# Sliding-window attention into a two-layer MLP: the first four blocks' biases on TensorE, and a new order of the first loads

## The chip, the cores and the metric

The kernel runs on one core of a Trainium2 chip. The metric is the device time of one execution in microseconds (us); each execution is timed, and the median of the runs stands for the kernel. One further execution was profiled.

## What is computed

Attention with 8 batches, 8 heads, 576 positions and a head size of 64, in which a query sees itself and the 127 positions before it, with a linear bias on the distance (ALiBi); then a two-layer MLP with a squared ReLU over the 4608 tokens. Inputs and output are float32.

```python
scores = scale * np.matmul(q, k.transpose(0, 1, 3, 2))        # scale = 1/8
rel = pos[:, None] - pos[None, :]
slopes = 2.0 ** (-8.0 * (np.arange(H) + 1) / H)
bias = slopes[:, None, None] * (-np.abs(rel))[None, :, :]
mask = (rel >= 0) & (rel < 128)
scores = np.where(mask, scores + bias[None], -1e9)
attn = softmax(scores)
x = (attn @ v) as [4608, 512]
h = x @ w_in                                                  # w_in [512, 2048]
r = np.maximum(h, 0.0)
out = (r * r) @ w_out                                         # w_out [2048, 512]
```

## The kernel before

**Tiling.** The 576 positions of a batch are cut into four blocks of 128 and one of 64, so there are 40 blocks. A block's queries need its own keys (the diagonal part) and those of the block before (the other part of the window). The first block of each batch has the diagonal part alone; these eight are blocks 0 to 7, done first. Blocks 0 to 3 are jobs of their own, 4 and 5, and 6 and 7, share one. The rest follow by pairs of batches: six full blocks, then two half blocks in one job.

**One block.** k and q of a block land side by side in a `kq` tile (128 positions by 1024). Both are transposed so that head channels lie on partitions: for blocks 0 to 7 by TensorE (`tp`, L470) with an eviction to `kqf` by ScalarE or VectorE (L291, L289), for later blocks by a DMA transpose that SP issues (`kqT`, L456). TensorE then writes scores to `s` (L526), keys on partitions and queries in columns, two heads at a time in two row groups. ScalarE writes `P` = exp(scale * s) (L550) in four instructions, VectorE multiplies `P` by `masks` (L558), which hold exp of the bias or 0. TensorE multiplies `P` by v with a column of ones (`pv`, L593, two halves of four heads); VectorE takes the reciprocal of the sum (L611) and scales (L615) into `x`. `x` is transposed into `xT`, by TensorE (`xp`, L635) for blocks 0 to 7 and by an SP DMA (L623) after.

**The MLP.** Nine groups of 512 tokens. For each, `h` (L718 for groups 0 to 2, whose units are 128 or 256 tokens wide, L735 after), then ReLU on ScalarE (`rt`, L683), the square on VectorE (`g`, L692), and `o` (L762), whose four parts of the hidden dimension need the four quarters of w_out in turn. A result tile `osb` is stored by SP (L786). `h` and `o` have two PSUM banks each, so only two output tiles are open at a time.

**Loads.** POOL issues the loads that cast float32 to bfloat16: blocks' k and q (L414), v (L419), w_in in four quarters of columns (L360), w_out in four quarters of rows (L363). `FIRST` gives their order at the start: block 0, 1, 2, w_in 0 and 1, w_out 0, block 3, w_in 2 and 3, and so on. Block 0's k and q (`N_HW = 1`) come another way: SP and ScalarE's queue load float32 halves into `stage` (L397) and VectorE casts them to `kq`.

**Order.** A planner in the kernel's own Python orders every instruction: each task has engines with a cost, a key, dependences, slots that it takes from rings and frees, and for a DMA a transfer time; the planner always starts the task that can start first on its engine, the key deciding within `NEAR` ns, and `ADJ` shifts single keys. Instructions are emitted in that order and each engine runs its own in order. Where the plan sees TensorE idle over 200 ns, `fill` puts matmuls on a zero tile `warm` there (L270).

Of the kernel before, what the change touches and what calls it, by code (L numbers as in the profile page):

```python
# [15 lines left out]
FIRST = ["b0", "b1", "b2", "i0", "i1", "o0", "b3", "i2", "i3", "o1", "o2", "o3", "b4", "b5", "b6", "b7"]  # L16
DIAG = [[0], [1], [2], [3], [4, 5], [6, 7]]
N_HW = 1
N_PE = 8
N_CUT = 1  # L20
N_PVH = 0
N_WARM = 8
FILL = 0.7
LEAD = 720
# [3 lines left out]
UNITS = {0: [(0, 128, 4), (128, 128, 4), (256, 128, 4), (384, 128, 4)], 1: [(0, 256, 2), (256, 256, 2)],  # L28
         2: [(0, 256, 2), (256, 256, 2)]}
PIECES = [4, 4, 4, 4]  # L30
# [5 lines left out]
    "e1.2": 99737.5, "e14.1": 197.91, "e16.2": -128.81, "e19.2": -8999803.95, "e2.3": -401.4, "e20.1": 2.03,  # L36
    "e3.1": 99809.35, "e6.3": 99108.3, "fc3.1": -547.61, "fc3.2": -237.14, "fc3.3": -684.14, "fc3.5": -652.43,
    "fc3.7": -100007.3, "fc3.8": -9000379.3, "m18.2": 165.47, "m18.3": -239.22, "n1.1": 100203.0, "n10.1": 495.17,
    "n12.1": 587.74, "n15.0": 308.11, "n16.0": 356.11, "n16.1": 706.81, "n9.0": 332.79, "o0.2.0": -103.48,
    "o0.2.1": -122.14, "o0.2.2": -99562.6, "o1.0.1": -100260.7, "o1.0.2": -100228.4, "o1.1.1": -99628.0,  # L40
    "o1.1.2": -152.7, "o1.1.3": -198.1, "o1.3.1": -99940.7, "o2.0.1": -99143.6, "o2.1.1": 200, "o2.2.0": -615.0,
    "oe1.0.0": -220.3, "ones2": 99179.7, "pv11.1": -99297.74, "pv19.0": -100068.55, "r18.0": 267.47, "r3.1": 99545.79,
    "relufc3.1": -100188.3, "relufc3.5": -99571.3, "reluu0.0.2": -99848.1, "reluu0.1.0": -100044.0,
    "reluu1.1.4": -579.61, "reluu2.0.5": -282.54, "squ0.0.0": -100027.7, "squ1.1.3": -388.31, "squ2.1.1": 40,
    "u0.2.0": -8999828.5, "u0.2.1": -99868.0, "u1.1.0": 39, "u1.1.1": -99305.4, "u1.1.4": -99991.3,
    "u1.1.6": -99367.7, "u2.0.5": -99873.0, "u2.0.6": -468.21, "u2.0.7": -99687.4, "u2.1.1": -187.45,
    "u2.1.2": -482.59, "u2.1.3": 39, "u2.1.7": -266.7,
# [24 lines left out]
class Plan:  # L72


    LAT = {"PE": 210.0, "ACT": 60.0, "DVE": 80.0, "POOL": 200.0, "SP": 200.0, "ACTQ": 200.0}
    BEGIN = {"POOL": 840.0, "SP": 740.0, "ACTQ": 740.0, "ACT": 2550.0, "DVE": 860.0, "PE": 1190.0}
# [4 lines left out]
    NEAR = {"PE": 25, "ACT": 60, "DVE": 25}  # L81
# [17 lines left out]
    def order(self):  # L99
# [37 lines left out]
        while len(done) < n_all:  # L137
# [40 lines left out]
            for u in t.users:  # L178
                left[u] -= 1
                at = st + dur if u.engs.keys() == {e} and t.dma is None else t.end  # L180
                if "SP" in u.engs and t.dma is None:
                    at += self.TO_SP
                u.ready = max(u.ready, at)
                if not left[u]:
                    for x in u.engs:
                        cand[x].append(u)
# [6 lines left out]
def kernel(  # L193
# [44 lines left out]
    masks = const.tile([128, H, 2, 128], BF16)  # L238
    dist = const.tile([128, 2, 128], FP32)
# [35 lines left out]
    def act(n):  # L275
        return n * 0.95 + 115.0

    def dve(n, rate=1):
        return n / rate / 0.96 + 180.0

    def dve_p(n, rate=1):
        return n / rate / 0.96 + 185.0
# [31 lines left out]
    t_ident = plan.add({"DVE": 230.0}, EARLY + 1, build_ident, [t_iota], name="ident")  # L314
# [7 lines left out]
    for part in (1, 0):  # L322
        key = EARLY + 2 if part else -1e5 + 1100
        t_dist[part] = plan.add({"DVE": 430.0}, key, lambda part=part: build_dist(part), [t_ident],
                                name=f"dist{part}", later=0.0 if part else 18000.0)
        for p in range(H):
            def build_mask(p=p, part=part):
                nc.scalar.activation(masks[:, p, part], dist[:, part], AF.Exp, bias=0.0,
                                     scale=-(2.0 ** (-8.0 * (head_at[p] + 1) / H)))
            t_mask[part].append(plan.add({"ACT": act(128)}, key + 1 + p, build_mask, [t_dist[part]], name=f"mask{part}.{p}"))  # L330

    def ones(ts):
        for t in ts:
            nc.vector.memset(t[:, :, D:D + 1], 1.0)
    t_ones = [plan.add({"DVE": 320.0}, EARLY + 3, lambda: ones(tiles["v0"][0:2]), name="ones0"),
              plan.add({"DVE": 900.0}, -1e5 + 300, lambda: ones(tiles["v0"][2:]), name="ones1", later=11000.0),
              plan.add({"DVE": 1200.0}, -1e5 + 900, lambda: ones(tiles["v"]), name="ones2", later=20000.0)]
# [4 lines left out]
    def zero():  # L342
        for m in halves:
            if m - B < size["v"]:
                nc.vector.memset(tiles["v"][m - B][64:128, :, 0:D], 0.0)
            if m - B < size["kqT"]:
                nc.vector.memset(tiles["kqT"][m - B][:, 0:C, 64:128], 0.0)
    t_zero = plan.add({"DVE": 1300.0}, -1e5 + 950, zero, name="zero", later=25000.0)
# [31 lines left out]
    def load_block(m, key):  # L380
# [10 lines left out]
        if split:  # L391
            stage = stages[m]
            t_l = []
            for i, src in enumerate((k, q)):
                for r, (eng, e) in enumerate((("SP", nc.sync), ("SP", nc.sync) if m else ("ACTQ", nc.scalar))):
                    def fetch(i=i, src=src, r=r, e=e):
                        e.dma_start(view(stage, i)[:, r], source(src, m, split)[:, :, r])  # L397
                    t_l.append(plan.add({eng: 740.0}, key + 0.1 * i, fetch, dma=330.0, lat=700.0 if i else 1650.0,
# [7 lines left out]
            engs = {"DVE": 480.0, "ACT": 600.0} if m else {"DVE": 480.0}  # L406
# [13 lines left out]
        l_v = plan.add({"POOL": 890.0}, key + 0.2, fetch_v, [t_zero] if kb == HALF else [], [s_v[m]],  # L420
                       dma=ns, name=f"lv{m}")
        t_v[m] = [l_v, t_ones[0 if m < 2 else 1 if m < B else 2]]
# [26 lines left out]
    def transpose_kq(m, due):  # L449
# [4 lines left out]
        if m >= N_PE:  # L454
            def flip():
                nc.sync.dma_start_transpose(out=tile_of(sT)[:, :, 0:n], in_=kq[s_kq[m].idx][0:n, :])  # L456
            t_f = plan.add({"SP": 1500.0}, due - 60, flip, t_kq[m] + [t_zero if kb == HALF else None], [sT],
                           [s_kq[m]], dma=1700.0 * n / 128, name=f"kqT{m}")
            t_kqT[m] = [[t_f], [t_f]]
            return  # L460
        t_tp, evs = [None, None], [[], []]
        for i in range(2):
# [13 lines left out]
            pieces = [(0, C // 2), (C // 2, C)] if i and m == 0 else [(0, C)]  # L476
            for c0, c1 in pieces:
                def evac(i=i, st=st, c0=c0, c1=c1, e=len(evs[i])):
# [4 lines left out]
                    else:  # L483
# [4 lines left out]
                                       [t_tp[i]] + evs[i], [], [st], name=f"ev{m}.{i}.{c0}"))  # L488
        last["tp"] = t_tp[1]
        t_kqT[m] = [[evs[0][0], evs[1][0]], evs[0] + evs[1]]  # L490

    def job(j, kind, ms, due):
        nb = len(ms)
        n = 64 if kind == "half" else 128
        for m in ms:
            transpose_kq(m, due)
        before = {m: at[seq[m][0], seq[m][1] - 1] for m in ms if kind != "diag"}
# [15 lines left out]
        bursts = [[0], [1]] if j == 0 else [[0, 1]]  # L513
        for z, grps in enumerate(bursts):
# [15 lines left out]
            for m in set(ms) | set(before.values()):  # L530
                deps += t_kqT[m][0] if z == 0 and len(bursts) > 1 else t_kqT[m][1]
# [11 lines left out]
        for i in range(4):  # L543
# [12 lines left out]
            def mask(w=w, flat=flat):  # L556
                if kind == "full" or (kind == "diag" and nb == 1):
# [13 lines left out]

    def values(j, kind, i, m, nb, sP, t_P, mb, due):
# [4 lines left out]
        if kind == "full":  # L577
            parts = [(slice(0, 128), mb), (slice(128, 256), m)]
        elif kind == "diag":
# [5 lines left out]
        for hf in range(2):  # L585
            sv = Slot("h" if j < N_PVH else "a")

            def pv(hf=hf, sv=sv):
                fill(t_pvs[hf], bank_of(sv, "pv"))
                for hi in range(4):  # L590
                    h = 4 * hf + hi
                    for w, mk in parts:
                        nc.tensor.matmul(sv.tile[0:n, hi * (D + 1):(hi + 1) * (D + 1)],  # L593
                                         Pt[sP.idx][:, place(h)].rearrange("p t q -> p (t q)")[:, w],
                                         tile_of(s_v[mk])[:, h, 0:D + 1], start=mk == parts[0][1], stop=mk == m)
            rel = []
            if hf:
                rel = [sP] + ([s_v[mb]] if mb is not None else []) + ([s_v[m]] if kb == HALF else [])
            t_pv = plan.add({"PE": 4 * len(parts) * 30.0 + 30}, due - 12 + hf, pv,
                            [last["pv"]] + t_P[2 * hf:2 * hf + 2] + [x for _, mk in parts for x in t_v[mk]],  # L600
# [11 lines left out]
            t_r = plan.add({"DVE": 200.0}, due - 12 + hf, rec, [t_pv], [sr], name=f"r{m}.{hf}")  # L612

            def norm(sv=sv, sr=sr, hf=hf):
                nc.vector.tensor_tensor(  # L615
                    xt[sx.idx][0:n, hf * 256:(hf + 1) * 256].rearrange("p (h e) -> p h e", h=4),
# [212 lines left out]
```

The softmax here doesn't subtract the row's maximum and nothing guards it: scores larger than these inputs give would overflow.

## Time and profile before

| | |
|---|---|
| median of 9 runs | 314.65 us (314.2 to 315.31) |
| the profiled execution | 314.65 us, its span 312.9 us |
| TensorE busy | 305.6 us, 98% of the span |
| ScalarE, VectorE, GpSimd busy | 173.3, 171.0, 105.6 us |
| DMA: POOL's queue q0 | 114,656 packets, 18.10 MB |
| DMA: SP's queue q1 | 50,592 packets, 20.65 MB |
| HBM read, written | 36.70 MB, 9.44 MB |

Some landings of POOL's loads, which arrive in the order of issue: v of block 0 at 6.53 us, k of block 1 at 7.37, v of block 2 at 11.59; w_in's quarters at 14.12, 17.08, 25.30 and 27.84; w_out's at 19.63, 30.42, 32.92 and 35.48; block 3's k, q, v at 20.48, 21.38, 22.21; q of block 7 at 45.54.

The page names engines PE (TensorE; PEld its weight loads), DVE (VectorE), ACT (ScalarE), POOL (GpSimd) and SP. Rows of digits cut the span into 40 slices of 7.8 us, each digit the busy share in tenths. A "releaser" is what ended an engine's wait. DMA queue rows give packets, MB and the time that packets took as a share of 16 engines. Matmul durations overlap, so costs of TensorE are read from start to start.

### The profile page before, as it was taken

To read this page: it belongs to the slowest core of one execution; us is meant where nothing else is said; L and a number is where in the kernel's file an instruction comes from. 1 tells how busy PE (TensorE), PEld (TensorE's weight loads), DVE (VectorE), ACT (ScalarE), POOL (GpSimd) and SP (SyncE) were. 2 spreads that over 40 slices of the span, in tenths; PEclk is the share of its full clock that TensorE was granted. 3 is DMA by queue.
4 is the path that set the end of the run, shared out by engine and by line. 5 is a ranking of instruction groups with operands and counts; after the bars stand their busy time and mean duration, and the time that the engine had idled before them with its cause. 6 is when DMAs were issued, how large, how long until landed. Compare 5 with 4: busy or idle time off the path is not lost.

```text
span 312.9 us, 7155 instructions
## 1 busy us (share of the span) xinstructions
PE 305.6 (98%) x2820; PEld 175.6 (56%) x2820; DVE 171.0 (55%) x492; ACT 173.3 (55%) x336; POOL 105.6 (34%) x131
## 2 busy tenths in 40 slices
PE   7989999999999999999999999999999999999996
PEld 3869757677766744455545554545454444444443
DVE  3757356667666665776666657666656222222211
ACT  4766566657677535855766554676564443444400
POOL 8843597462624864201937203600000000000000
PEclk9999999999999999999999999999999999999999
DMA  9999999999999999967999979991220100110022
GB/s 127 186 191 205 172 175 190 133 164 148 212 146 191 205 165 200 139 82 138 149 174 164 176 85 129 176 196 52 51 69 17 69 34 35 37 34 34 34 96 73
DMA packets 165714, 39.54 MB, mean 126 GB/s; under 512 B 156336, under 2 KB 161200, under 8 KB 165680
## 3 DMA queue, kind: packets, MB, share of 16 engines
q0 software_dynamic: 114656, 18.10, 81.4%
q1 hardware_dynamic: 50592, 20.65, 35.5%
q8 instruction: 22, 0.36, 0.5%
q10 hardware_dynamic: 432, 0.33, 0.4%
q14 instruction: 12, 0.10, 0.1%
HBM read 36.70 MB, written 9.44 MB: 147 GB/s over the span
## 4 chain that ended last, share of the span: by engine, by line
PE 83%; DMA 10%; POOL 5%; issue 1%; ACT 0%; POOLq 0%; SPq 0%
PE o L762 35%; PE h L735 27%; PE h L718 10%; PE pv L593 5%; PE s L526 5%; DMA w_in_sb<-in_moe_w_in_dram 4%; DMA kqT<-kq 3%; POOL kq L414 3%; DMA kq<-in_q_dram 3%; POOL vf L419 1%; POOL w_in_sb L360 0%; POOL vt L419 0%; POOL w_out_sb L363 0%; POOL dist L305 0%; ACT osb L291 0%
## 5 line engine op out<-in xcount | busy, mean ns | idle before, releaser
L762 PE MATMUL o<-w_out_sb,g 128*128 128x512 bf16 (+2 forms) x592 | 142.7, 373 | 0.4 <-DMA w_out_sb<-in_moe_w_out_dram 0.4
L683 ACT ACTIVATE rt<-h 128x512 bf16<-128x512 f32 x144 | 85.6, 607 | 91.8 <-PE h L735 69.4
L692 DVE TENSOR_TENSOR g<-rt 128x512 bf16<-128x512 bf16 x144 | 59.9, 421 | 73.9 <-ACT rt L683 73.3
L735 PE MATMUL h<-xT,w_in_sb 128*128 128x512 bf16 x384 | 96.2, 379 | 0.0
L762 PEld LDWEIGHTS <-g 128*128 128x128 bf16 x592 | 54.1, 98 | 56.0 <-issue 0.5
L550 ACT ACTIVATE P<-s 128x512 bf16<-128x512 f32 (+1 forms) x136 | 67.3, 582 | 18.1 <-PE s L526 18.1
L735 PEld LDWEIGHTS <-w_in_sb 128*128 128x128 bf16 x384 | 35.3, 98 | 39.5
L558 DVE TENSOR_TENSOR P<-P,masks 128x512 bf16<-128x512 bf16 (+1 forms) x112 | 44.4, 404 | 16.4 <-ACT P L550 11.9
L718 PE MATMUL h<-xT,w_in_sb 128*128 128x128 bf16 (+1 forms) x512 | 46.7, 246 | 1.1 <-DMA w_in_sb<-in_moe_w_in_dram 1.1
L414 POOL DMA_DIRECT2D kq<-in_k_dram x39 | 33.4, 856 | 40.1 <-DMA kqT<-kq 33.0
L718 PEld LDWEIGHTS <-w_in_sb 128*128 128x128 bf16 x512 | 38.4, 98 | 6.2 <-DMA w_in_sb<-in_moe_w_in_dram 1.4
L419 POOL DMA_DIRECT2D vt<-in_v_dram x32 | 27.2, 853 | 41.9 <-PE pv L593 37.3
L414 POOL DMA_DIRECT2D kq<-in_q_dram x39 | 33.7, 864 | 7.9 <-DMA vt<-in_v_dram 3.2
L615 DVE TENSOR_TENSOR x<-pv,rec 128x256 bf16<-128x256 f32 (+1 forms) x80 | 33.4, 421 | 2.5 <-DVE rec L611 0.2
L593 PEld LDWEIGHTS <-P 128*128 128x128 bf16 (+1 forms) x576 | 25.1, 101 | 13.0 <-DVE P L565 1.3
L291 ACT ACTIVATE osb<-o 128x512 f32<-128x512 f32 (+1 forms) x23 | 13.6, 593 | 21.0 <-PE o L762 21.0
L611 DVE RECIPROCAL rec<-pv 128x4 f32<-128x4 f32 (+1 forms) x80 | 14.0, 178 | 19.2 <-PE pv L593 17.5
L593 PE MATMUL pv<-vt,P 128*128 128x65 bf16 (+1 forms) x448 | 23.8, 194 | 0.0
L526 PEld LDWEIGHTS <-kqT 64*128 64x128 bf16 x448 | 12.4, 94 | 8.2 <-issue 7.4
L289 DVE COPY osb<-o 128x512 f32<-128x512 f32 (+1 forms) x14 | 9.5, 682 | 13.4 <-PE o L762 12.9
L526 PE MATMUL s<-kqT 64*128 64x128 bf16 (+1 forms) x256 | 15.6, 209 | 0.0
L526 PE MATMUL s<-kqT,kqT 64*128 64x128 bf16 (+1 forms) x192 | 11.4, 210 | 0.3 <-DMA kqT<-kq 0.3
(41 smaller groups left out, 98.9 us busy)
## 6 DMA issues: line engine op xcount, KB each, us to landing
out_dram<-osb SPq DMA_DIRECT2D x31, 256.0 KB, 3.7
kq<-in_k_dram POOLq DMA_DIRECT2D x31, 128.0 KB, 6.9
kq<-in_q_dram POOLq DMA_DIRECT2D x31, 128.0 KB, 6.9
vt<-in_v_dram POOLq DMA_DIRECT2D x24, 128.0 KB, 7.8
w_in_sb<-in_moe_w_in_dram POOLq DMA_DIRECT2D x4, 512.0 KB, 10.7
w_out_sb<-in_moe_w_out_dram POOLq DMA_DIRECT2D x4, 512.0 KB, 15.6
vf<-in_v_dram POOLq DMA_DIRECT2D x8, 128.0 KB, 6.6
out_dram<-osb SPq DMA_DIRECT2D x8, 128.0 KB, 2.3
```

What stands on the lines that cost most here:

```text
L414: nc.gpsimd.dma_start(view(kq[s_kq[m].idx], i), source(src, m, split))
L419: nc.gpsimd.dma_start(tile_of(s_v[m])[0:n, :, 0:D], source(v, m))
L526: nc.tensor.matmul(sS[2 * g2 + r].tile[:, jj * 256 + c0:jj * 256 + c0 + w], tile_of(s_kqT[mk])[rows, c, :], tile_of(s_kqT[mq])[rows, C + c ...
L550: nc.scalar.activation(flat(Pt[sP.idx]), sS[i].tile.rearrange("p (j t) -> p j t", j=2)[:, :, lo:hi], AF.Exp, bias=0.0, scale=scale)
L558: nc.vector.tensor_tensor(flat(Pt[sP.idx]), flat(Pt[sP.idx]), flat(masks), op=ALU.mult)
L593: nc.tensor.matmul(sv.tile[0:n, hi * (D + 1):(hi + 1) * (D + 1)], Pt[sP.idx][:, place(h)].rearrange("p t q -> p (t q)")[:, w], tile_of(s_v ...
L615: nc.vector.tensor_tensor(xt[sx.idx][0:n, hf * 256:(hf + 1) * 256].rearrange("p (h e) -> p h e", h=4), heads(sv)[0:n, :, 0:D], sr.tile[0:n ...
L683: nc.scalar.activation(srt.tile[:, 0:n], slot.tile[:, 0:n], AF.Relu, bias=0.0, scale=1.0)
L692: nc.vector.tensor_tensor(o, i, i, op=ALU.mult)
L718: nc.tensor.matmul(slot.tile[:, f * w:(f + 1) * w], w_in_sb[:, cc, fc * 128:(fc + 1) * 128], xT[:, cc, lo:lo + w], start=cc == 0, stop=cc ...
L735: nc.tensor.matmul(slot.tile, w_in_sb[:, cc, fc * 128:(fc + 1) * 128], xT[:, cc, g * 512:(g + 1) * 512], start=cc == 0, stop=cc == C - 1)
L762: nc.tensor.matmul(slot.tile[:, 0:hi - lo], gt[:, fc, t * 128:(t + 1) * 128], w_out_sb[:, fc, lo:hi], start=fc == 0, stop=fc == FCB - 1)
```

## The change

Blocks 0 to 3 get a job kind of their own, `lone`. Before their scores, TensorE multiplies the identity by `slopes`, which holds bias / scale (and a very large negative number outside the mask), into the same two PSUM banks that the scores are added to. One exponential per bank of 512 columns follows, and no multiply by a mask. `slopes` is built by VectorE or ScalarE at the start; `masks` are still needed from block 4 on and are built later. Block 1's k and q are now loaded like block 0's, four more issues on SP, with casts by VectorE or ScalarE. Block 3 is loaded ahead of the weights, w_in's first quarter in two pieces, and w_out's quarters alternate with w_in's. The planner's latency of ScalarE and VectorE after an instruction is split from its cost, and the tasks' costs are new. `ADJ` is another list.

```diff
-FIRST = ["b0", "b1", "b2", "i0", "i1", "o0", "b3", "i2", "i3", "o1", "o2", "o3", "b4", "b5", "b6", "b7"]
+FIRST = ["b0", "b1", "b2", "b3", "i0", "i1", "o0", "i2", "o1", "i3", "o2", "i4", "b4", "o3", "b5", "b6", "b7"]
-N_HW = 1
+N_HW = 2
-N_CUT = 1
-N_PVH = 0
+N_CUT = 2
+N_PVH = 2
+N_EV = 3
-LEAD = 720
+LEAD = 640
-UNITS = {0: [(0, 128, 4), (128, 128, 4), (256, 128, 4), (384, 128, 4)], 1: [(0, 256, 2), (256, 256, 2)],
+UNITS = {0: [(0, 128, [2, 2, 4, 4, 4]), (128, 128, [4, 4, 4, 4]), (256, 128, [4, 4, 4, 4]), (384, 128, [4, 4, 4, 4])],
-PIECES = [4, 4, 4, 4]
+PIECES = [2, 2, 4, 4, 4]
...
-    LAT = {"PE": 210.0, "ACT": 60.0, "DVE": 80.0, "POOL": 200.0, "SP": 200.0, "ACTQ": 200.0}
+    LAT = {"PE": 210.0, "ACT": 180.0, "DVE": 190.0, "POOL": 200.0, "SP": 200.0, "ACTQ": 200.0}
+    SELF = {"ACT": 120.0, "DVE": 110.0}
-    NEAR = {"PE": 25, "ACT": 60, "DVE": 25}
+    NEAR = {"PE": 0, "ACT": 250, "DVE": 25}
...
-                at = st + dur if u.engs.keys() == {e} and t.dma is None else t.end
+                at = st + dur + self.SELF.get(e, 0.0) if u.engs.keys() == {e} and t.dma is None else t.end
...
     def act(n):
-        return n * 0.95 + 115.0
+        return n * 0.832 + 51.0
     def dve(n, rate=1):
-        return n / rate / 0.96 + 180.0
+        return n / rate / 0.96 + 55.0
...
+    t_slope = [[], []]
+    for r in range(2):
+        for c in range(4):
+            def build_slope(r=r, c=c):
+                f = -(2.0 ** (-8.0 * (2 * c + r + 1) / H)) / scale
+                o = slopes[:, r * 4 + c]
+                t = t_slope[r][c]
+                if t.eng == "DVE":
+                    nc.vector.tensor_single_scalar(o, dist[:, 1], f, op=ALU.mult)
+                else:
+                    nc.scalar.activation(o, dist[:, 1], AF.Copy, bias=0.0, scale=f)
...
-            engs = {"DVE": 480.0, "ACT": 600.0} if m else {"DVE": 480.0}
+            engs = {"DVE": 350.0, "ACT": 480.0} if m else {"DVE": 350.0}
...
-            pieces = [(0, C // 2), (C // 2, C)] if i and m == 0 else [(0, C)]
+            pieces = [(0, C // 2), (C // 2, C)] if m < N_EV else [(0, C)]
...
+        if kind == "diag" and nb == 1:
+            lone(j, ms[0], due)
+            return
...
+    def lone(j, m, due):
+        sS = [Slot("a") for _ in range(2)]
+        def biases():
+            for r in range(2):
+                nc.tensor.matmul(bank(sS[r], f"s{r}"), ident,
+                                 slopes[:, 4 * r:4 * r + 4].rearrange("p c q -> p (c q)"), start=True, stop=False)
+        t_b = plan.add({"PE": 2 * mm(512)}, due - 33, biases, t_slope[0] + t_slope[1] + [t_ident, last["s"]], sS,
+                       name=f"b{m}")
+        def scores():
+            for c in range(C):
+                for r in range(2):
+                    rows = slice(64 * r, 64 * r + 64)
+                    nc.tensor.matmul(sS[r].tile[:, c * 128:(c + 1) * 128], tile_of(s_kqT[m])[rows, c, :],
+                                     tile_of(s_kqT[m])[rows, C + c, :], start=False, stop=c == C - 1)
+        t_s = plan.add({"PE": 190.0 + 4 * mm(128)}, due - 32, scores, [t_b] + t_kqT[m], name=f"s{m}")
...
+            def expo(r=r):
+                nc.scalar.activation(lone_P(sP)[:, r * 512:(r + 1) * 512], sS[r].tile, AF.Exp, bias=0.0, scale=scale)
...
-                    h = 4 * hf + hi
+                    h = 2 * hi + hf if kind == "lone" else 4 * hf + hi
```

In the new order of instructions, POOL's loads begin with v of block 0, v of block 1, block 2, block 3, the two half pieces of w_in, w_out's first quarter, and then in turn w_in, w_out, w_in, w_out, w_in, block 4, w_out, blocks 5, 6 and 7. SP issues the first two output stores, the first `kqT`, a store, the second `kqT`, a store, and two more `kqT`; before, three stores stood ahead of the first three `kqT`. TensorE has 25 fillers where it had 76.

## The prediction, made before the result was known

> **What bounds the kernel now.** I read the page first (busy shares and the rows by slices), then who TensorE waits for, then the chain of work that ended last, then DMA packets in half microseconds, then TensorE's timeline. The page, parts 1 and 2:
>
> ```profile
> span 312.9 us, 7155 instructions
> ...
> PE   7989999999999999999999999999999999999996
> ...
> DMA  9999999999999999967999979991220100110022
> ```
>
> TensorE is full from the fourth slice on (23 us); only the stretch before has room. The DMA row is full from the first slice. TensorE's waits in the whole run (us in total, times, longest):
>
> ```profile
> PE wm L440 <- DVE warm L309: 1.2, 1, 1.2
> PE h L718 <- DMA w_in_sb<-in_moe_w_in_dram: 1.1, 2, 0.8
> PE tp L470 <- DVE kq L289: 1.0, 1, 1.0
> PE o L762 <- DMA w_out_sb<-in_moe_w_out_dram: 0.4, 1, 0.4
> PE s L526 <- DMA kqT<-kq: 0.3, 1, 0.3
> PE pv L593 <- ACT P L550: 0.3, 1, 0.3
> ```
>
> Only 0.3 us of `h` (at 25.35) and the 0.3 us of `s` (at 62.58) fall after 25 us. Filler matmuls on `warm` (L270, 76 of them) hide the rest of the early idling. The chain, in order of time (start, us, what):
>
> ```profile
> 9.98 1.76 POOL kq L414 x2
> 12.53 12.77 DMA w_in_sb<-in_moe_w_in_dram
> 25.35 3.75 PE h L718 x64
> ...
> 44.07 8.14 DMA kq<-in_q_dram
> 52.26 10.28 DMA kqT<-kq
> ```
>
> Two DMA arrivals pin TensorE: w_in's third quarter ("i2", lands 25.30) and, while TensorE is full, the keys and queries of blocks 7 to 9 that come just in time.
>
> So I count TensorE's work and call what is left of the clock "lost time". Prices are back-to-back starts in the timeline: 64 `h` of 128 columns 3.57 us (55.8 ns each), 4 `o` 0.86, 8 `tp` 0.44, 16 `s` 0.55, 8 `pv` 0.24, 4 `xp` 0.22. Before 25.35 the kernel does 96 `h` 5.36, 8 `o` 1.72, 32 `tp` 1.76, 32 `s` 1.10, 24 `pv` 0.72, 12 `xp` 0.66: 11.3 us, so 14.0 us are lost. At the transposes of block 7 (45.91) work is 31.7, lost 14.2; the stall at 62.58 makes it 14.5, and no wait follows. The work of both kernels is equal but for fillers and biases, so the time changes by lost time alone.
>
> **The change, part by part.**
>
> Multiplies by masks (L558) of blocks 0 to 3 go: 16 x 0.29 = 4.7 us of VectorE. The 16 exponentials of 256 columns become 8 of 512: four back to back took 1.21 us (7.66 to 8.87), two of 0.61 take the same, so ScalarE gains nothing. Added: 8 `slopes` instructions before block 0 (nearest rows 0.22 to 0.30 each, six on VectorE, about 1.4 us between 1.9 and 3.7, where it idled 1.8 us for `stage`), and 8 bias matmuls of 512 columns, 8 x 0.216 = 1.7 us. The biases stand where 76 fillers (6.2 us) stood and 25 remain, so they cost nothing; without that cover, 1.7 us. The 16 `masks` (16 x 0.21 = 3.4 us) move behind the first exponentials. Block 0's chain shortens by about one multiply, 0.3 us, and its `x` was ready at 10.97, three us ahead of the first w_in piece (14.12): hidden. So are the evictions cut in halves (0.39 on ScalarE, 0.29 on VectorE, beside one another, for one of 0.60 or 0.42) and the memsets made separate tasks (0.065 each).
>
> Block 1's k and q leave POOL's queue for SP's: two POOL issues of 0.88 us and two transfers of 0.84 us less (landings there are 0.84 apart), four SP issues of about 0.75 and four HW transfers of 128 KB more, then two casts (0.43 to 0.67 each) on ScalarE and VectorE. Behind SP's issues nothing waits before 39 us. What the HW packets take from POOL's stream, from 5 to 5.5 us and then from 5.5 to 6:
>
> ```profile
> q0 software_dynamic: 386, 0.05, 152.9%
> q1 hardware_dynamic: 58, 0.05, 37.6%
> ...
> q0 software_dynamic: 612, 0.08, 242.7%
> ```
>
> While q1 sent 58, q0 sent 226 fewer, 3.9 per packet; 4 x 144 packets cost 2,250 of 1,224 a us, 1.8 us. From 43 to 44 us an output store's 100 packets of up to 2 KB cost 588, 5.9 each; for 1 KB I halve it: 512 x 2.95 / 1,224 = 1.2 us. Both rows are near; I take 1.5 (1.2 to 1.8). Against 1.68 saved, the queue as a whole is 0.2 us ahead.
>
> The Trainium skill (DMA: Bandwidth & Descriptors, section Queues, rings and completion order) says that an engine serves queue rows in turn, packet by packet. That speaks against adding HW loads while POOL's queue drains. The rows show fewer HW than POOL packets (58 to 386), so SP's supply, not the turn, sets the share; by strict turns block 1 would land sooner, and the sum would stay, since each packet still costs its time.
>
> Block 3's k, q, v are moved ahead of the weights, and w_out's second quarter ("o1") ahead of i2. i2 therefore lands 2.53 (o1) - 1.68 + 1.5 later, plus 0.1 for two smaller pieces instead of one (twice the packets; bounds 0 and 0.2): 25.30 + 2.45 = 27.75. But all four blocks are then ready, and before that unit TensorE's new order has 128 `h` 7.14, 12 `o` 2.58, 32 `tp` 1.76, 32 `s` 1.10, 32 `pv` 0.96, 16 `xp` 0.88: 14.4 us. Lost there: 27.8 - 14.4 = 13.4, 0.6 less than now. TensorE gets there in time: block 3's q takes the seventh place of POOL's loads, where v of block 2 landed at 11.59, so 13.1; block 0 needs 2.2 us from cast (6.39) to `pv` (8.54), and with the cast's place taken by two evictions I allow 2.8, so the first `h` at 15.9 (the first w_in piece lands at 11.59 + 0.84 + 1.27 + 1.5 = 15.2). From there 10.1 us of work and some 0.6 for w_out's first quarter end at 26.6: 1.1 us of cover for late exponentials.
>
> This is not kept, because the next arrivals bind. Queue order from there is o2, i3, block 4, o3, blocks 5 to 7: the same set that had landed by 45.54 (q of block 7: issued 38.61, 6.9 us). TensorE's two looks at block 7:
>
> ```profile
> 43.25 0.61 PE L470 MATMUL tp<-ident,kq 128*128 128x128 bf16 x8
> ...
> 45.91 0.61 PE L470 MATMUL tp<-ident,kq 128*128 128x128 bf16 x8
> ```
>
> (The first is block 6.) Now there are 0.4 us to spare at block 7. In the new order its second four transposes come after 256 `h` 14.28, 48 `o` 10.32, 60 `tp` 3.30, 48 `s` 1.65, 32 `pv` 0.96, 16 `xp` 0.88: 31.4 us, at 13.4 lost due at 44.8. q lands at 45.54 - 1.68 + 1.5 + 0.1, plus what a second output store takes before it. Two output tiles now finish one behind the other at about 40 us; a store cost 588 packets, 0.5 us; I take 0.2 (0 to 0.5): 45.66. Lost: 45.7 - 31.4 = 14.3 (bounds 13.7 to 14.9). Against 14.5: 0.2 us gained.
>
> After that the transposed keys must come in time. Scores of block 8 stand after 41.7 us of work, 2.2 fewer than now (43.9), so they are due at 56.0; kqT of block 8 lands now at 58.03. It is issued at 48.19 behind two output stores (45.60, 46.37, landing 51.07, 52.09), and the new SP order puts only the two stores of about 40 us ahead of it. The next transposes land 4.5 and 3.8 us after the one before them, so alone it lands by 48.3 + 4.5 to 6, 53 to 54.5: hidden by 1.5 us. Blocks 9 to 12 are due at 62.7, 66, 72 and 81 and landed at 62.5, 66.4, 71.4 and 80.8 behind that late one; with it earlier they have 1.5 us or more, and the 0.3 us stall at 62.58 goes (counted above). Later attention runs ahead (block 38's scores after 191 us of work instead of 217); the chain from a `pv` through `x`, SP and the kqT keeps 5 us or more, since those transfers wait for TensorE's own progress. The planner's new issue and latency figures cost no instruction; they are this order.
>
> Filling fewer gaps bears on the clock: eight warm matmuls took 3.59 us before 4.8 us, and back to back 0.216 each later; the profile's row of granted clock reads 9 in every slice, with TensorE's waits up to 1.2 us. The skill (TensorE: Matmul & The Clock Gate, section What's actually happening) has the clock halve after an idle window of about 3.4 us. I see no such gap in the new order; if one came, the matmuls after it would take twice as long, and the early cover of about 13 us would hide most of that.
>
> Sum: 312.9 - 0.2 = 312.7 us of span; the profiled execution took 314.65, equal to the median of the runs shown, 1.75 more than its span. Forecast: **314.4 us**. A difference under 0.2% (0.63 us) can't be told from none.
>
> **Rivals.** (A, forecast) Early gain eaten by block 7's arrival: 13.7 to 14.9 lost, 313.85 to 315.05.
>
> (B) The queue is not the bound at block 7: HW loads use the queue's half-idle ramp (3 to 5.5 us) and the stores come later. For it: from 4 to 4.5 us q0 sent 186 of 612. Then i2 sets lost time, 13.4 less up to 0.5: 0.8 to 1.6 us gained, 313.05 to 313.85, say **313.4**.
>
> (C, slower) kqT of block 8 stays late. Scores of block 8 come 2.2 us of work sooner; if their keys still land at 58.03, TensorE stalls 2.0 us there, lost 16.3 against 14.5: **316.4**. It decides from a landing of 56.2 on, a microsecond each. For it: 9.85 us from issue to landing now; against it: the stores ahead of it are gone.
>
> (D) The change does not do what it says: multiplies leave an engine that nobody waited for (TensorE waited 0.0 us for L558), the order gives what it costs, 314.65. It lies inside A's range and is counted there.
>
> **How the numbers follow.** A with D 0.60, B 0.20, C 0.17, others 0.03. A is faster (below 314.02) in 0.18, within in 0.35, slower (above 315.28) in 0.07; B is faster; C slower in 0.16, within in 0.01; of the others 0.01 is faster and 0.02 slower. Faster 0.39, same 0.36, slower 0.25. A's own range is 313.85 to 315.05; to leave no more than 2 in 10 out it must reach most of B and the nearer part of C: 313.1 to 315.8.
>
> **What would show it.** Right: the third w_in quarter landing near 27.7 with lost time near 13.4, then a wait of `tp` for block 7's q near 45.7; `s` of block 8 without a wait. Wrong: no wait of `tp` and block 7 transposed by 44.9 (B); a wait of `s` for `kqT` near 56 to 58 (C); a first w_in piece later than 16 us, or block 1's casts after 11 us; half clock after 5 us.

## The result, and the profile after

The changed kernel takes 317.27 us (median of 10 runs, 314.99 to 318.07) against 314.41 for the kernel before beside it (32 runs): ratio 1.0072, 95% interval 1.0056 to 1.0089. It is slower, and outside the predicted range. Its runs spread over 3 us, the other's over 2. The profiled execution took 317.96 us.

The page of the changed kernel, parts 1 and 2:

```profile
span 315.5 us, 7080 instructions
...
PE   7899999999999999999999899999999999999995
...
DMA  9999999999999999999999999822011100010122
```

TensorE still looks full; of the lost 2.6 us of span only one 8 shows after the start, in the slice from 174 to 181 us. But the DMA row is now full for 25 slices (197 us) without the thinner places that it had from the 18th: attention runs ahead, and its loads with it. TensorE's waits:

```profile
PE wm L470 <- DVE warm L313: 1.2, 1, 1.2
PE s L559 <- DVE x L689: 0.8, 1, 0.8
PE s L620 <- DVE kqf L293: 0.8, 2, 0.5
...
PE tp L500 <- DMA kq<-in_q_dram: 0.7, 1, 0.7
...
PE s L559 <- DMA kqT<-kq: 0.3, 1, 0.3
PE o L836 <- DVE g L765: 0.3, 1, 0.3
```

In each row the first number is the sum of the waits in us, the second their count, the third the longest. The waits for `w_in` are gone. New are `s` waiting for a vector instruction on `x` (L689, the normalise), and `o` waiting for `g` (at 27.57 us). The chain in order of time names the transfers behind these waits:

```profile
41.91 7.40 DMA kq<-in_q_dram
49.37 7.58 DMA kqT<-kq
...
65.32 7.93 DMA kqT<-kq
...
165.82 8.17 DMA xT<-x
```

Lost time, counted as in the prediction (start of a matmul minus TensorE's work before it; the prediction's own prices for that work give 0.1 to 0.3 us more in the columns up to 46 us). The last column is the time from the last matmul to the end of the span:

| us | 25 | 46 | 62 | 100 | 160 | 180 | 300 | end |
|---|---|---|---|---|---|---|---|---|
| before | 13.9 | 13.95 | 14.1 | 14.55 | 15.3 | 15.5 | 16.0 | 3.25 |
| after | 13.4 | 13.9 | 15.2 | 15.7 | 16.2 | 17.3 | 18.0 | 3.8 |

The gain of 0.5 at 25 us is there and is gone by 46, but not as forecast: 0.4 of it goes at 27.57 us, where `o` waits for `g` and starts 0.4 late, before block 7 comes into play. Then the new kernel loses 1.3 us between 46 and 62 (0.8 at block 7's transposes, whose q lands at 46.36; 0.4 at the scores of block 8, whose keys land at 56.95), where the other loses 0.15. It keeps that distance to 160 us, loses 1.0 at 174.5, and 0.6 more after the last matmul.

At 174.5 us the stall has three links: `s` needed a PSUM bank, the normalise that frees it waited 2.2 us for one of the three `x` tiles, and that tile was held by an `xT` transpose that took 8.17 us to land.

### The profile page after: what moved, and what is told of

Same layout as the page of the kernel before. It is cut to its first block, busy times and chain, and to the rows that moved or that the text cites. A ratio compares the mean times of both kernels' runs of the same rounds, so it can differ in the third digit from the quotient of the medians.

```text
span 315.5 us, 7080 instructions
## 1 busy us (share of the span) xinstructions
PE 305.6 (97%) x2777; PEld 174.1 (55%) x2777; DVE 167.3 (53%) x498; ACT 169.4 (54%) x324; POOL 104.4 (33%) x130
## 4 chain that ended last, share of the span: by engine, by line
PE 80%; DMA 13%; POOL 3%; ACT 1%; DVE 1%; issue 1%; POOLq 0%; SPq 0%
PE o L836 36%; PE h L809 26%; PE h L792 9%; DMA kqT<-kq 5%; PE pv L663 5%; PE s L559 4%; DMA w_out_sb<-in_moe_w_out_dram 3%; DMA xT<-x 3%; DMA kq<-in_q_dram 2%; POOL kq L444 1%; POOL vf L449 1%; ACT P L583 1%; POOL w_in_sb L390 0%; DVE g L765 0%; DVE x L689 0%
## 5 line engine op out<-in xcount | busy, mean ns | idle before, releaser
L756 ACT ACTIVATE rt<-h 128x512 bf16<-128x512 f32 (+1 forms) x145 | 86.1, 602 | 90.3 <-PE h L809 67.1
L765 DVE TENSOR_TENSOR g<-rt 128x512 bf16<-128x512 bf16 (+1 forms) x145 | 60.4, 418 | 91.5 <-ACT rt L756 90.3
L583 ACT ACTIVATE P<-s 128x512 bf16<-128x512 f32 x120 | 62.6, 606 | 16.8 <-PE s L559 16.8
L591 DVE TENSOR_TENSOR P<-P,masks 128x512 bf16<-128x512 bf16 x96 | 40.2, 421 | 14.9 <-ACT P L583 10.9
L689 DVE TENSOR_TENSOR x<-pv,rec 128x256 bf16<-128x256 f32 (+1 forms) x80 | 31.8, 416 | 6.5 <-DMA xT<-x 6.0
L663 PEld LDWEIGHTS <-P 128*128 128x128 bf16 (+1 forms) x576 | 23.7, 101 | 10.2 <-DVE P L591 0.8
L295 ACT ACTIVATE osb<-o 128x512 f32<-128x512 f32 (+1 forms) x21 | 12.2, 582 | 21.1 <-PE o L836 21.1
L663 PE MATMUL pv<-vt,P 128*128 128x65 bf16 (+1 forms) x448 | 21.9, 194 | 0.0
L293 DVE COPY osb<-o 128x512 f32<-128x512 f32 (+1 forms) x16 | 10.9, 683 | 14.2 <-PE o L836 14.1
L559 PE MATMUL s<-kqT 64*128 64x128 bf16 (+1 forms) x256 | 15.7, 209 | 0.0
L680 DVE RECIPROCAL rec<-pv 128x4 f32<-128x4 f32 (+1 forms) x80 | 12.3, 171 | 5.3 <-PE pv L663 4.5
## 6 DMA issues: line engine op xcount, KB each, us to landing
w_out_sb<-in_moe_w_out_dram POOLq DMA_DIRECT2D x4, 512.0 KB, 14.3
w_in_sb<-in_moe_w_in_dram POOLq DMA_DIRECT2D x3, 512.0 KB, 15.3
```

The source lines that it names most:

```text
L559: nc.tensor.matmul(sS[2 * g2 + r].tile[:, jj * 256 + c0:jj * 256 + c0 + w], tile_of(s_kqT[mk])[rows, c, :], tile_of(s_kqT[mq])[rows, C + c ...
L583: nc.scalar.activation(flat(Pt[sP.idx]), sS[i].tile.rearrange("p (j t) -> p j t", j=2)[:, :, lo:hi], AF.Exp, bias=0.0, scale=scale)
L591: nc.vector.tensor_tensor(flat(Pt[sP.idx]), flat(Pt[sP.idx]), flat(masks), op=ALU.mult)
L689: nc.vector.tensor_tensor(o, heads(sv)[0:n, :, 0:D], sr.tile[0:n, :].unsqueeze(2).to_broadcast([n, 4, D]), op=ALU.mult)
L756: nc.scalar.activation(srt.tile[:, 0:n], slot.tile[:, 0:n], AF.Relu, bias=0.0, scale=1.0)
L765: nc.vector.tensor_tensor(o, i, i, op=ALU.mult)
```

## The experiments

All experiment kernels take the planner's order and write it out engine by engine, with named tasks moved (a pair in MOVES puts the first behind the second on its engine) or with a part of the order taken from the other kernel. So the planner can't reshuffle the rest (e8 and e16 alone have the start planned anew). The medians are of 4 to 12 runs; the ratio is to runs of the kernel before timed beside them.

| run | median us | ratio to before, 95% |
|---|---|---|
| e1 five x tiles | 316.6 | 1.0058 (1.0032 to 1.0084) |
| e2 block 7's transposes later | 317.12 | 1.0081 (1.0062 to 1.0100) |
| e3 attention later | 336.11 | 1.0687 (1.0657 to 1.0717) |
| e4 multiplies, order kept | 322.67 | 1.0240 (1.0221 to 1.0260) |
| e5 old start, new rest | 318.6 | 1.0134 (1.0115 to 1.0153) |
| e6 new start, old rest | 316.28 | 1.0065 (1.0044 to 1.0085) |
| e7 = e6, block 1 on POOL | 317.03 | 1.0069 (1.0054 to 1.0085) |
| e8 = e6, multiplies | 316.73 | 1.0064 (1.0045 to 1.0083) |
| e9 = e6, join moved | 317.39 | 1.0107 (1.0081 to 1.0133) |
| e10 = e9, last semaphore | 316.74 | 1.0070 (1.0047 to 1.0094) |
| e11 = e9, new order from 112 us | 320.47 | 1.0177 (1.0144 to 1.0210) |
| e12 new start, old rest from 54 us | 315.70 | 1.0027 (1.0009 to 1.0046) |
| e13 = e12, last semaphore | 314.84 | 1.0005 (0.9984 to 1.0026) |
| e14 = e1, x ahead of keys | 316.24 | 1.0034 (1.0013 to 1.0056) |
| e15 = e14, last semaphore | 315.33 | 1.0012 (0.9990 to 1.0034) |
| e16 = e13, multiplies | 315.92 | 1.0028 (1.0013 to 1.0044) |
| e17 = e13, block 1 on POOL | 315.36 | 1.0016 (1.0001 to 1.0032) |

**Single stalls (e1 to e4).** Five `x` tiles:

```diff
+REAL = {'x': 5}
...
-    xt = ring("x", size["x"], [128, d_model])
+    xt = ring("x", REAL["x"], [128, d_model])
```

> The changed kernel with five x tiles instead of three, every engine's order as it was. Theory (the 1.1 us stall of s at 174 us is VectorE's normalise waiting for a free x, because attention runs ahead and its xT transposes take 8 us beside the loads): no wait of L689 for 'xT<-x', no jump of lost time at 174, 317.3 - 1.1 = 316.2 us. Rival (the late transposes delay h or the next keys anyway): the stall shows up again under another name, 317.0 to 317.5.

The wait at 174 us was gone, but the profiled run had another, in TensorE's waits:

```profile
PE h L839 <- DMA xT<-x: 3.1, 1, 3.1
```

It stands at 82.85 us: the first `h` of group 2 needs `xT` of block 9, and it landed at 82.71 (80.48 in the changed kernel's profile, with 0.14 us to spare; 76.00 before, with 2.11). The 12 runs went from 314.96 to 319.25. So the ring was one place of several, and what an execution loses differs from one to the next; the interval of e1 overlaps that of the changed kernel.

Block 7's transposes behind the values of blocks 4 and 5:

```diff
+MOVES = [('tp7.0', 'pv5.1'), ('tp7.1', 'tp7.0')]
```

> The changed kernel with TensorE's two groups of transposes of block 7 moved past four o and twelve pv (1.6 us of work); nothing else is moved. Theory (TensorE is held to the arrivals one after the other): the 0.8 us wait for q of block 7 goes, but scores of block 8 then wait 0.8 us longer for their keys, which land at 56.95 as before; lost time after 57 us stays 15.2, 317.1 to 317.4. Rival (each stall counts by itself): 0.8 us faster, 316.5.

The time did not move, as the theory had it, though by another wait: block 7's own wait went, and 0.86 us came back at 49.6 us, `xp` for `x`, since block 7's eviction now held VectorE's queue ahead of those normalises. The profiled execution (315.23) was one with no other stall, and its lost time at the last matmul was 15.96, that of the kernel before: up to there the new order can be as fast, when every transfer is in time.

All scores and values from block 8 on two units later on TensorE, as well as these moves (one list, cut after its first pairs):

```diff
+MOVES = [('tp7.0', 'pv5.1'), ('tp7.1', 'tp7.0'), ('s8', 'o1.0.1'), ('pv8.0', 'o1.1.0'), ('pv8.1', 'pv8.0'), ('s9', 'u1.1.7'),
...
```

> As the run before, and all scores and values from block 8 on stand two units of h or o (1.74 us of work) later in TensorE's order. Theory: scores of block 8 are then due about 57.9 to 58.5, after their keys (56.95); lost time after 57 us is 14.0 instead of 15.2, and the x stall at 174 us stays, 317.3 - 1.2 = 316.1. Rival (the values and scores that follow run short of cover when moved, or loss before 57 us is not what makes the time): 317.0 or more.

19 us slower than the changed kernel, and of no use for the question. TensorE's waits show why:

```profile
PE h L856 <- ACT rt L803: 8.5, 10, 1.4
PE h L839 <- ACT rt L803: 3.8, 3, 1.4
```

ScalarE's queue still had the exponentials where they were. Each now waited for its late scores with the relus behind it, and `h` waited for those. An order is one thing over all engines.

Biases taken away, the multiply sent from the place of `pv`:

```diff
-                nc.tensor.matmul(bank(sS[r], f"s{r}"), ident,
-                                 slopes[:, 4 * r:4 * r + 4].rearrange("p c q -> p (c q)"), start=True, stop=False)
+                bank(sS[r], f"s{r}")
+                if m == 0:
+                    nc.scalar.activation(emask[:, r], slopes[:, 4 * r:4 * r + 4].rearrange("p c q -> p (c q)"),
+                                         AF.Exp, bias=0.0, scale=scale)
...
+                if kind == "lone":
+                    p = lone_P(sP)[:, hf * 512:(hf + 1) * 512]
+                    nc.vector.tensor_tensor(p, p, emask[:, hf], op=ALU.mult)
```

> The changed kernel with the biases of blocks 0 to 3 taken away again: scores start their own banks, two exponentials make a mask from the slopes, and VectorE multiplies each half of 512 columns by it; the order is otherwise kept. Theory (biases stand in idle time, the multiplies were hidden): lost time at 46 us within 0.3 of 13.9, 317.0 to 317.6. Rival 1 (eight bias matmuls of 0.22 us cost TensorE): 1.7 us faster, 315.6. Rival 2 (the biases shorten the start, and their gain is hidden by other losses): the first h later by 1 us or more and the time 0.5 to 1.5 us slower.

5 us slower than the changed kernel, more than any theory had. `pv` waited 4.5 us in seven places for the multiplies, which this edit puts late in VectorE's queue. The granted clock was also lower here: the page's row of it reads

```profile
PEclk9578999999999999999999999999999999999999
```

(0.50 from 9.5 to 16.4 and from 19.8 to 26.6 us), and the mean over the span was 0.968 to 0.979 in all four runs. So the 5 us are not the waits alone. The run says that the order leaves no room there, not what the biases are worth (e16).

**Start against rest (e5 to e8).** The start of one kernel's plan and the rest of the other's, on all engines. `ORDER` is the list of all tasks with their engines, written out; it follows the one plan for tasks up to 46 us and the other behind them, and the kernel emits it as it stands:

```diff
+        if ORDER:
+            got = [x.split(":") for x in ORDER.split()]
...
+            for name, eng in got:
+                by[name].eng = eng
...
```

> The kernel before up to 46 us of the plan (all its instructions, and every engine's order, as they were), then every engine in the changed kernel's order. Theory (the loss comes from the order after block 7, where keys of blocks 8 to 11, the xT of blocks 9 and 11 and the x ring have 0 to 1 us to spare where they had 2 to 5): 316.0 to 317.5, runs spread over 3 us. Rival (the loss comes from the new start: HW loads, biases, blocks before weights): 314.2 to 314.9.

Rival C of the prediction alone: the scores of block 8 stand 2.2 us of work sooner, and the keys are as late as before (58.67). TensorE's wait, and then busy times and granted clock (the column after the engines) of the stretches around it:

```profile
PE s L719 <- DMA kqT<-kq: 2.6, 1, 2.6
```

```profile
58.70:60.40 1.70, 1.69 (x25) 1.37 (x25) 0.58 (x2) 1.27 (x3) 1.13 (x2) 0.85 1.71 138
60.40:62.20 1.80, 1.80 (x6) 0.70 (x5) 1.54 (x4) 1.28 (x3) 0.88 (x1) 0.50 1.47 205
62.20:64.20 2.00, 2.00 (x21) 1.60 (x20) 0.32 (x3) 0.44 (x1) 0.81 (x1) 0.72 2.02 171
64.20:66.20 2.00, 2.00 (x33) 1.85 (x32) 1.94 (x8) 0.76 (x2) 0.94 (x2) 1.00 1.64 157
```

The stall took lost time from 14.2 to 17.0, and then the clock was granted at 0.50 for a while and it went on to 18.6. A stall of 2.6 us cost 4.4. The median, 318.6 (one of five runs took 325.89), lies above the theory's 317.5: the later order loses what the theory gave it and more.

> The changed kernel up to 46 us of the plan (biases, HW loads of block 1, blocks before weights, its orders), then every engine in the order of the kernel before. Theory (loss in the later order alone): lost time 13.7 to 14.0 at 46 us and no more after it than in the kernel before, 314.0 to 314.9. Rival (the new start costs): 316.0 or more.

Lost time 13.6 at 46 us, then one wait, and none after it:

```profile
PE xp L903 <- DVE x L884: 1.3, 1, 1.3
```

From there lost time rises by 1.6 to 300 us, no more than in the kernel before. But the wait is at the join, where the one order passes into the other: the old order has `xp4.0` right behind values that the new start has moved. The median, 316.28, is the rival's number and not the theory's; so the size was open until e12.

Block 1 by POOL's queue, and blocks 0 to 3 with multiplies that the planner places:

```diff
+                for i, src in enumerate((k, q)):
+                    nc.gpsimd.dma_start(kq[s_kq[m].idx][:, i * d_model:(i + 1) * d_model].rearrange("s (h d) -> s h d", h=H),
+                                        source(src, m))
```

> As e6, and k and q of block 1 are loaded by POOL's queue again, ahead of block 1's v, without stage and casts; the order is kept. Theory (HW loads took 2.0 us from POOL's stream and saved it 1.7): q of block 7 lands 0.3 us earlier than in e6, lost time at 46 us lower by 0 to 0.3, time that of e6 or 0.3 less. Rival (HW packets use room that POOL's stream leaves): q of block 7 lands 1.7 us later, 1.0 to 1.7 us slower than e6.

```diff
+            t_M.append(plan.add({"DVE": dve(512, 2)}, due - 31 + r, mult, [t_P[r], t_em[r]], name=f"mm{m}.{r}"))
```

> As e6, and blocks 0 to 3 without biases: scores start their own banks, the mask comes from two exponentials of the slopes, and VectorE multiplies each half of 512 columns (8 multiplies, placed by the planner, unlike e4); order from 46 us on as in e6. Theory (the arrival of q of block 7 sets the lost time, whatever a start up to 1 us later does): lost time at 46 us within 0.3 of e6, time within 0.4 of e6. Rival (the biases earn their place on the chain of blocks 0 to 3, and the start counts): 1.0 us or more slower than e6.

By their times neither differs from e6, but e6 has its wait at the join and e8 has not. The 16.0 that e8 had lost at 46 us missed the theory's 0.3 around e6's 13.6. Both were done again on a clean join (e16, e17).

**The join and the end (e9 to e13).**

```diff
+MOVES = [('tp7.0', 'pv5.1'), ('tp7.1', 'tp7.0'), ('o0.3.0', 'tp7.1'), ('oe0.0.0', 'n5.1')]
```

> As e6 (new start, old order from 46 us on), and at the join the places that the kernel before gave them: the two transposes of block 7 and the first part of output tile 3 (o0.3.0) behind the values of blocks 4 and 5, the eviction oe0.0.0 behind VectorE's normalises of block 5. Theory (e6's 1.4 us wait of xp for x was the join's alone, and the later order of the kernel before has no other stall): lost time after 50 us 13.7 to 14.1, 316.3 - 1.3 = 315.0; still 0.6 above a perfect gain because the end after the last landing takes 1.7 instead of 1.1 us. Rival (the new start itself brings a loss that is only named xp there): 316.0 or more.

A miss: 0.9 us of wait of `xp` for `x` stayed, and 0.5 of `pv` for P came. The eviction `ev7.1.0` stood ahead of the normalises in VectorE's queue, as in e2, and the moved transposes held it back.

> As e9, and six of the late output stores (groups 5 and 6) are issued in two halves, which puts the last store on the eighth of the eight completion semaphores of the HW DMAs instead of the first. Theory (SyncE waits at the end for the lanes in turn, 62 ns each; in the changed kernel eight of these waits stand behind the last store's, in the kernel before four): last landing to end of span 1.7 - 7 x 0.062 = 1.27 us, time 0.4 below e9. Rival (the end is as long whichever lane comes last, and the 0.6 us are POOL's barrier): as e9 within 0.1.

```diff
-                (nc.scalar if final else nc.sync).dma_start(
+                cuts = [(lo, hi)] if (g, t) not in SPLIT else [(lo, 256), (256, hi)]
+                for x, y in cuts:
+                    (nc.scalar if final else nc.sync).dma_start(
...
```

The records of SyncE's semaphore instructions after the last store has landed (us from that landing):

```
before  0.02 0.08 0.14 0.20 | 0.26 drain | end of span 1.10
after   0.01 0.07 0.14 0.20 0.26 0.32 0.38 0.44 | 0.51 drain | end of span 1.71
e10     0.02 | 0.08 drain | end of span 1.28
```

SyncE waits for eight HW DMA semaphores in a fixed turn, 62 ns each. Transfers take the semaphores in rotation, so the four HW loads that the change adds shift the last store from the fifth to the first (SyncE issues 106 transfers in the kernel before, 110 in the changed one): four more waits behind it, 0.25 us. In e10 SyncE issues 117 (one of the six halved stores was two transfers already), the last store is on the eighth, and the end is 0.43 shorter, as computed; the medians of e9 and e10 differ by 0.65, with intervals that overlap. The other 0.35 us of the longer end lie between POOL's semaphore instructions (0.40 us between two that stood 0.09 apart before); e7 has them without the HW loads, e5 has not. Their cause is open.

> As e9, with the changed kernel's order again from 112 us on. Theory (attention that runs ahead meets a full ring of x at 174 us and has 3 to 6 us to spare for its keys): stalls of 0 to 1.1 us, 0 to 1.1 us slower than e9, with a wider spread of the runs. Rival (only the stretch from 46 to 112 us costs): as e9 within 0.2.

3 us slower than e9, more than expected, and from 318.2 to 321.5. The profiled execution was the fastest of them. Its waits at the join are those of e9 (0.9 of `xp`, 0.5 of `pv`); beyond them it has 0.4 us for keys at 64.9 us, in the old order's stretch, 0.3 of `s` for ScalarE's `P` at 120.6 us, and pieces under 0.25 us. Where the slower runs lose, no profile here shows.

> As e6, but the changed kernel's order is kept up to 54 us of the plan, past its own values of block 6, and the old order follows from there; nothing is moved at the join. Theory (the stretch behind block 7 in the new order costs about 1.5 us, the start only its longer end of 0.6): lost time after 58 us 14.0 to 14.7 (0 to 0.8 us of wait for q of block 7), no wait of TensorE after it, 314.9 to 315.7, runs within 1.5 us. Rival (the new start costs by itself, e6 and e9 were no accident of the join): 316.2 or more.

> As e12, with the last store on the last of the eight HW completion semaphores (as in e10). Theory: last landing to end 1.28 us instead of 1.71, 0.4 below e12: 314.5 to 315.3. Rival (the end does not show in the time): as e12.

(e12 takes the old order from 54 us of the plan on, where e6 took it from 46; e13 adds the split of e10.) This settles where the loss is. With the old order from 54 us on, the only waits of TensorE that show in e12's lost time after 25 us are 0.3 of `o` for `g` at 28.6 and this one at 63.6:

```profile
PE s L754 <- DMA kqT<-kq: 0.2, 1, 0.2
```

Lost time in e13 is 14.0 at 46 us, 14.2 at 62 and 15.9 at 300 (before: 13.95, 14.1, 16.0), and its time is that of the kernel before. (Its last store is on the eighth semaphore and that of the kernel before on the fifth, which is worth 0.2 us to it.) The changed kernel is 0.72% slower; by the ratios 0.45% goes with the order behind 54 us (e12; the intervals don't touch), and 0.22% with the place of the last store (e13; the profiles have 0.4 us, 0.14%, and the intervals overlap).

**Why the new order is late (e14, e15).** SyncE's issues around 70 us in the changed kernel:

```profile
65.32 1.24 SPq L486 DMA_TRANSPOSE kqT<-kq  x1
66.65 1.49 SPq L696 DMA_TRANSPOSE xT<-x  x1
72.07 1.23 SPq L486 DMA_TRANSPOSE kqT<-kq  x1
73.40 3.59 SPq L696 DMA_TRANSPOSE xT<-x  x2
```

The normalise of block 9 ended at 71.28. Its `xT` was issued at 73.40, because the keys of block 12 stand ahead of it in SyncE's queue, and they waited for their q, which landed at 72.02. In e1 the two were 70.72 and 73.90.

```diff
+MOVES = [('x9', 'x8'), ('x11', 'st1.0.0')]
```

> The changed kernel with five x tiles (as e1), and in SyncE's queue the transpose of x of block 9 stands ahead of the keys of block 12, that of block 11 ahead of the keys of block 15. Theory (x of block 9 is ready at 71.3 but stands 2.1 to 3.2 us behind the keys of block 12, whose issue waits for their load; so h of group 2 waits at 80 us, 0.2 us in one run and 3.1 in another): x of block 9 issued within 1 us of its normalise, no wait of h for xT, 315.2 to 316.2, and the runs spread over less than 2 us instead of 4. Rival (the packets' contention sets when xT lands, whichever is issued first): as e1, 316.6 and a spread of 4 us.

> As e14, with the last store on the last of the eight HW completion semaphores. Theory: 0.4 below e14, 314.8 to 315.8. Rival: as e14.

In e14 `xT` of block 9 went out at 71.66 and landed at 78.61:

```profile
66.64 6.21 SPq L743 DMA_TRANSPOSE xT<-x  x2
72.95 1.25 SPq L533 DMA_TRANSPOSE kqT<-kq  x1
```

No `h` waited at 80 us, nothing at 174, and the medians came to 316.24 and, with the last semaphore, 315.33. The spread was 3.0 and 2.3 us, not under 2. What is left (0.5 at block 7, 0.5 at the keys of block 8, 0.4 us at 184 in e14's profile and at 118 in e15's) are again waits for transfers or for what stands behind them. The intervals of e1 and e14 overlap, so the times alone don't show the gain; the trace shows that the queue's order held `xT` back.

**The start again (e16, e17).** The edits of e8 and e7 on e13.

> As e13, but blocks 0 to 3 have no biases: two exponentials of the slopes make the mask and VectorE multiplies (as in e8; the start is planned anew, the old order follows from 50 us on). Theory (the bias is worth 2 us to the start of this order, and by 46 us block 7 no longer hides it: e8's lost time there was 16.0 against 13.6): lost time at 46 us 15.5 to 16.2, 316.3 to 317.0. Rival (as the prediction had it, a start up to 1 us later is hidden by the arrival of block 7's q): lost time at 46 us within 0.5 of e13's 14.0, within 0.5 of 314.8.

> As e13, but k and q of block 1 come by POOL's queue (as e7; the last store is on the last semaphore here too). Theory (HW loads cost POOL's stream about what they take off it): v of block 3 lands within 0.3 us of e13's, time within 0.4 of e13's 314.8. Rival 1 (HW loads cost 0.5 us or more net): 314.3 or less. Rival 2 (they save their 1.7 us): 316 or more.

Without biases the lost time is 15.5 at 46 us, where e13 has 14.0, and the median is 1.1 us above e13's: below the theory's 316.3, above the rival's 315.3. Part of it is the granted clock, which fell to 0.50 at 9.45 us for 3.4 us in e16's profile:

```profile
9.00:10.00 1.00, 0.85 (x11) 0.85 (x12) 0.41 (x2) 1.00 (x3) 1.00 (x3) 0.73 2.02 192
10.00:11.00 1.00, 1.00 (x14) 1.00 (x13) 0.68 (x3) 0.43 (x2) 0.73 (x1) 0.50 2.40 156
```

Four of its twelve runs had a mean granted clock of 1.0 and took 315.26 to 315.53; the eight at 0.993 to 0.995 took 315.89 to 316.65. Of e13's twelve runs, eleven had 0.998 or more. So about half of the 1.1 us goes with the lower clock, which the start without biases met more often; and its start is planned anew and joined at 50 us, so the rest is not the biases' alone either.

With block 1 on POOL's queue v of block 3 lands at 13.96 instead of 14.24, and the time is 0.5 above e13's with intervals that overlap: neither rival, and the theory not told from a small loss.

## Why the prediction was wrong, by its own steps

- Right in kind: the wait of `tp` for block 7's q. It came at 46.36 us (forecast 45.66), so that by the prediction's prices 15.0 us were lost there, just above its bounds (14.3, 13.7 to 14.9). Four other profiles of the same start (e1, e2, e13, e15) have that q at 45.53 to 45.64, as the sum had it. At w_in's third quarter, forecast for 27.75 with 13.4 lost, the data landed at 28.32, and the first `h` on it began at 28.44 with 14.0 lost by the same prices, after `o` had waited for `g`. The first `h` of all came at 16.8, not 15.9, inside the cover that the sum gave it.
- Wrong, and the first to decide: "alone it lands by 48.3 + 4.5 to 6, 53 to 54.5: hidden by 1.5 us". The issue was at 49.37, since q of block 8 landed at 49.32, and the transpose took 7.58 without a store ahead of it, 56.95 in all. I took the spacing of two landings (4.5 and 3.8) for the time that one takes; from issue to landing the first four keys of the kernel before took 8.2 to 10.3, all of them beside POOL's loads. Those issued from 138 to 143 us in the changed kernel, where the loads pause, took 3.2 to 4.0. Rival C stated the mechanism and its threshold (56.2); 0.17 was too little for it, and its price left out the clock (e5). It prices this one place, 0.4 us of the 2.8 that the span is over.
- Wrong: "Blocks 9 to 12 ... have 1.5 us or more". The profile after has 0.75, 0.05, 0.04 and 3.3.
- Wrong, and the largest term: "the chain from a `pv` through `x`, SP and the kqT keeps 5 us or more, since those transfers wait for TensorE's own progress". They wait for SyncE's queue, in which an `xT` stands behind keys that wait for a load on POOL's queue (e14). `xT` of blocks 9, 11 and 16 had 0.14, 0.20 and 1.2 us to spare (before: 2.1, 3.6, 3.1), and the ring of three `x` was full at 174 us while an `xT` took 8.17 to land; with five (e1) that wait was gone. "Attention runs ahead" was counted as cover; it moves the loads forward too, and so takes quiet stretches in which transposes were quick: POOL issues no load from 131.5 to 147.3 and from 175.9 to 192.6 us in the kernel before, from 130.6 to 143.2 and from 174.4 to 181.2 in the changed one.
- Not in the sum: the end of the program, 0.6 us longer (e10).
- Open: the price of block 1's HW loads to POOL's stream, taken at 1.5 us (1.2 to 1.8) against 1.68 saved. v of block 3 landed 0.28 us later in e13 than in e17, which makes 2.0, but 0.19 earlier in e6 than in e7, which makes 1.5; and executions with the same loads up to there differ by more (13.90 in e15, 14.80 in e14).
- "So ScalarE gains nothing" and "the biases ... cost nothing": without them this order is 1.1 us slower (e16), some half of it by the lower clock, and the arrival of block 7 does not hide that. What the biases alone are worth stays open; e13 shows the start as a whole even.
- The two sums side by side: predicted span 312.7, measured 315.5. The difference of 2.8 us is 0.7 at block 7, 0.4 at the keys of block 8, 1.0 at 174.5, 0.6 at the end, and 0.1 in small pieces.

## What to carry to other kernels

Where a new order brings work forward, list for each transfer when its data is ready, what stands ahead of it in its queue and what that waits for, and how long it took in the busiest stretch: the spare time of each against its first use is the quantity that changes, and it does not show in waits until it is gone. The order here, with many transfers 0 to 1 us in time, is slower in the median and spreads, even where its best run (314.99) is near the old one's median (314.41). Moving one engine's instructions without those of the engines that it feeds makes new waits (e2, e3, e9).

## What the runs showed of the hardware, unexpected

- A stall of 2.6 us was followed, some 1.2 us after TensorE had started again, by a granted clock of 0.50 for 3.4 us, and the loss grew by 1.6 us (e5; the mean of 0.85 from 58.7 to 60.4 us puts the fall at about 59.9). The Trainium skill (TensorE: Matmul & The Clock Gate, section What's actually happening) gives an idle window of about 3.4 us; here less was enough. In the start of e12, where TensorE was busy for 0.43 of the 2 us from 6 to 8, it came as well, and lost time at 25 us was 14.5 against 13.15 in e13, the same instructions there (e12's rows below). The busy time of that stretch does not decide it: in e16 TensorE was busy for 1.04 us from 6 to 8 and the clock fell at 9.45; in e13 it was busy for 0.92 and the clock did not fall.

```profile
8.00:12.00 4.00, 3.29 (x37) 2.23 (x37) 2.11 (x12) 2.29 (x5) 3.42 (x5) 0.86 2.17 179
12.00:16.00 4.00, 4.00 (x47) 2.87 (x46) 2.60 (x9) 2.50 (x6) 3.01 (x5) 0.71 1.81 182
```

- The place of the last store among eight semaphores is worth up to 0.43 us at the end, 62 ns each.
